# Soft-MoE on a gated recurrence: the combine's turned logits in SBUF, their difference on GpSimd, fewer fillers, and new orders

## The chip, the cores and the metric

One NeuronCore of a Trainium2 chip runs the whole kernel as one launch. The metric is the device time of one execution in microseconds (us). Before the change it is 282.06 us, the median of three runs (281.35 to 282.72). PE is TensorE, DVE is VectorE, ACT is ScalarE, POOL is GpSimd, SP is SyncE.

## What is computed

All arrays are float32. The first half is a gated linear recurrence over 4 sequences of 5056 tokens with 256 channels; the second is a soft mixture of 8 experts with 4 slots each over all 20224 tokens.

```
log_a   = 8 * sigmoid(r_gate) * log(clip(sigmoid(a_param), 1e-6, 1 - 1e-6))
a       = exp(log_a)
h[t]    = a[t] * h[t-1] + sqrt(max(1 - a[t]^2, 1e-6)) * sigmoid(i_gate[t]) * x[t]     # y = h, restarted for each sequence
logits  = y @ phi                                   # 20224 x 32
d       = exp(logits - max over tokens) ; d /= sum over tokens + 1e-9
slots   = d.T @ y                                   # 32 x 256, 4 rows to an expert
out_e   = relu(slots_e @ w1_e) @ w2_e               # hidden width 1024
c       = exp(logits - max over slots) ; c /= sum over slots + 1e-9
result  = c @ out                                   # 20224 x 256
```

## The kernel before, in words

The tokens are cut into quads of 512 (the last of 256), numbered 0 to 39. A unit is what one load brings: quad 0 alone, then pairs of quads, and quad 39 alone; 21 units, 0 to 20. A group, of which there are 12, is two units (groups 0 to 8) or one (9 to 11). r_gate comes with channels on partitions, x and i_gate with tokens on partitions. Nearly all of SBUF is one array, `all_s`, of 48 slots, which the program's allocator gives out; beside it there are four buffers `yn` for the recurrence's output with tokens on partitions. PSUM's eight banks are two single banks and three pairs, and eight single banks once the last pairs are free.

Every step is a task with a name, made of a few letters and a number: a load `Dr3`, `Di3` or `Dx3` of unit 3; `SR` and `SI`, the gates' sigmoids, as hyperbolic tangents (ScalarE); `EX`, the exponential that makes a (ScalarE); `SQ`, its square (GpSimd or VectorE); `RT`, the root (ScalarE); `U`, the product of input gate and x (GpSimd or VectorE); `TU`, its turn into PSUM (PE); `ST`, times the root, and `SC`, the scan (VectorE); `TY`, the turn of the scan's output (PE) and `YC`, its copy to `yn` (ScalarE or VectorE); `LG`, the logits (PE); `LE`, their copy with a running maximum (VectorE); `LD`, `TE`, `ES`, the difference, its turn and its exponential; `AC`, the sum over tokens on PE, `DM` and `AE`, its correction to a new maximum. A letter per quad in the string `IV` says how U is made: D is one operation on VectorE, (i + 1) * x; E is the plain product i * x, and TU then turns both the product and x into the same bank, which adds them; P adds 1 to i on GpSimd first.

Behind the last group stands the merge: the maxima are turned and joined (`MT`, `MX`, `MR`, `MC`), the weights of the partial sums made (`WJ`, `WE`, `W`), and the slots computed (`SP`, copied by `SL`, L1281). The experts follow: `L1.0` to `L1.7`, the first product of each expert (PE, L1320), `HS`, `HT`, `HR`, the relu with a turn, in two halves; `L20.x` and `L21.x`, the second product for either half of the channels (PE, L1368); `SO` (L1386), `RS` (L1391) and `SW` (L1395), the output rows scaled, spread over the partitions and copied.

The combine runs on each group g: `CT` turns blocks of the logits on VectorE (L1428), `CM` takes the maximum over the slots (L1439), `CS` subtracts it (L1442), `CE` is the exponential (ScalarE, L1445), `RR`, `RB`, `RC` make the reciprocal of the sum (L1457 to L1459), `CN` multiplies by it (GpSimd, L1462), and `HE` turns the result back (VectorE, L1484). Then for each half of the channels, u = 2g and 2g + 1: `OT` (PE, L1498), its copies `OE` from PSUM (ScalarE L1512 or VectorE L1514), and the transfer `OD` out (SyncE, L1525). In the kernel before, CT writes to a PSUM bank.

The order of the work on every engine is written out as a list of task names for each, and one list, B, for the order in which buffers are taken. A planner walks through these lists with an estimated duration for each task and emits the instructions; at run time every engine works through its own in that order and waits on semaphores. Where the planner sees PE idle, between two given times (`WARMF` and `WARMT`), it puts in a filler: two transposes of the identity that no one reads (L1206). SyncE issues all loads and outputs; `a_param` alone is loaded from ScalarE's queue (L678). The program's functions that the change touches are these:

Of the kernel before, what the change touches and what calls it, by code (L numbers as in the profile page):

```python
# [15 lines left out]
P = 128  # L16
# [10 lines left out]
IV = 'DDDEEEEEEEDEEEEEEEEEEEEEEDEEEEPPEPPPPPPP'  # L27
# [12 lines left out]
WARMT = 245.0  # L40
# [37 lines left out]
GATES0 = False  # L78
# [19 lines left out]
    ),  # L98
    "ACT": (
# [11 lines left out]
    ),  # L111
# [43 lines left out]
COLDX = 1.9  # L155
IDLE = 2.8
CHILL = 5.0
LOAD = 1.41

EXG = 2  # L160

MI = ()
SI2 = ()
RT2 = ()
XFER = 1.265
ISSUE = 0.4
FIRST = 0.7
REACH = 2.6
REACHO = 1.55
LATO = 1.75  # L170
LATL = 1.1
DEEP = 8
PEX = 1.03

ODS = 0
OHALF = 1

# [373 lines left out]
def kernel(  # L551
# [11 lines left out]
    nc = tc.nc if tc is not None else None  # L563
# [6 lines left out]
    QT = J * P  # L570
# [72 lines left out]
    add = planner.add  # L643
# [493 lines left out]
    def exs(p):  # L1137

        return [] if p < first_of[p][-1] else [("EX", first_of[p][0], h) for h in range(H)]
# [464 lines left out]
```

## Time and profile before

| what | value |
|---|---|
| median of 3 runs | 282.06 us (281.35 to 282.72) |
| the profiled execution's own time | 281.48 us |
| its span, first to last instruction | 279.3 us |
| mean granted PE clock | 0.936 of full |
| busy: PE, DVE, ACT, POOL | 237.8, 235.3, 234.0, 181.2 us |
| HBM read, written | 78.94 MB, 20.71 MB |
| chain that ended last | PE 25%, POOL 24%, DVE 19%, ACT 12%, DMA 9%, issue 6% |

The span cut into 40 equal slices of 7 us, each digit the busy share in tenths (PEclk: the granted clock in tenths of full speed):

```profile
PE   8979688777699798798998999999999999989910
...
DVE  0066999999989999999999999999999999986420
ACT  6799999999999999999999999998823388697420
POOL 5102979999999999899999999998210430222000
PEclk9999799979979989999999999999999999999555
DMA  7999999999999969939699999999940069999995
```

A busy time is that of an engine's instructions; matmuls overlap, so PE's is no measure of its peak. The span holds the loads and the recurrence (to about 205 us), the merge and the experts (to about 222), and the outputs.

### The profile page before, as it was taken

How to read it: one execution, taken by the hardware profiler on the slowest of the kernel's cores; microseconds unless marked ns; L12 is line 12 of the kernel's file. 1: busy time of each engine (PE TensorE's matmuls, PEld its weight loads, DVE VectorE, ACT ScalarE, POOL GpSimd, SP SyncE). 2: the span in 40 equal slices, each digit the busy share in tenths (PEclk: the TensorE clock that was granted, in tenths of full speed). 3: DMA queues.
4: the chain of work that ended last, by engine and by line, in shares of the span. 5: the costliest groups of instructions: out<-in, count | busy, mean ns of one | idle time of the engine just before them, and what ended most of it. 6: DMA issues, size and time to landing. Idle time of an engine off the chain costs nothing.

```text
span 279.3 us, 5879 instructions
## 1 busy us (share of the span) xinstructions
PE 237.8 (85%) x2405; PEld 178.9 (64%) x2405; DVE 235.3 (84%) x279; ACT 234.0 (84%) x237; POOL 181.2 (65%) x143
## 2 busy tenths in 40 slices
PE   8979688777699798798998999999999999989910
PEld 8979576655476686476766776857665766545600
DVE  0066999999989999999999999999999999986420
ACT  6799999999999999999999999998823388697420
POOL 5102979999999999899999999998210430222000
PEclk9999799979979989999999999999999999999555
DMA  7999999999999969939699999999940069999995
GB/s 255 412 422 422 422 414 420 421 420 425 392 422 418 428 248 422 427 113 407 223 400 374 391 395 413 414 407 428 419 170 2 2 238 415 411 425 420 406 413 246
DMA packets 15562, 100.02 MB, mean 358 GB/s; under 512 B 1968, under 2 KB 2480, under 8 KB 4144
## 3 DMA queue, kind: packets, MB, share of 16 engines
q1 hardware_dynamic: 15392, 99.65, 87.7%
q8 instruction: 19, 0.31, 0.4%
q14 instruction: 7, 0.06, 0.0%
q10 hardware_dynamic: 144, 0.00, 0.0%
HBM read 78.94 MB, written 20.71 MB: 357 GB/s over the span
## 4 chain that ended last, share of the span: by engine, by line
PE 25%; POOL 24%; DVE 19%; ACT 12%; DMA 9%; issue 6%; SPq 0%; ACTq 0%; DVEq 0%; POOLq 0%
POOL all_s L822 10%; POOL all_s L839 10%; DVE all_s L920 10%; DVE pair L903 6%; PE bank L1498 5%; DMA all_s<-in_x_dram 4%; PE pair L943 3%; POOL all_s L810 3%; ACT all_s L854 3%; DMA out_dram<-all_s 3%; DMA all_s<-in_r_gate_dram 3%; PE bank L1206 3%; PE bank L1320 3%; PE pair L885 2%; ACT all_s L800 2%
## 5 line engine op out<-in xcount | busy, mean ns | idle before, releaser
L920 DVE TENSOR_TENSOR_SCAN all_s<-all_s,pair 128x1024 f32<-128x1024 f32 (+8 forms) x48 | 92.8, 1950 | 0.7
L822 POOL TENSOR_TENSOR all_s<-all_s 128x1024 f32<-128x1024 f32 (+1 forms) x35 | 81.4, 2348 | 4.5 <-ACT all_s L800 3.1
L839 POOL TENSOR_TENSOR all_s<-all_s 128x1024 f32<-128x1024 f32 (+2 forms) x36 | 66.9, 1878 | 22.6 <-ACT all_s L854 21.8
L885 PE MATMUL pair<-ident,all_s 128*128 128x128 f32 x524 | 69.1, 286 | 11.5 <-DVE all_s L920 7.0
L885 PEld LDWEIGHTS pair<-ident,all_s 128*128 128x128 f32 x524 | 60.5, 146 | 22.8 <-DVE all_s L920 9.2
L903 DVE SCALAR_TENSOR_TENSOR pair<-all_s,pair 128x1024 f32<-128x1024 f32 (+2 forms) x42 | 48.0, 1151 | 3.8 <-ACT all_s L868 2.1
L943 PE MATMUL pair<-ident,all_s 128*128 128x128 f32 x312 | 42.1, 279 | 6.1 <-DVE all_s L920 4.7
L943 PEld LDWEIGHTS pair<-ident,all_s 128*128 128x128 f32 x312 | 34.3, 141 | 14.6 <-DVE all_s L920 6.8
L854 ACT ACTIVATE all_s<-all_s,ca 128x2048 f32<-128x2048 f32 (+3 forms) x24 | 42.2, 1788 | 0.1
L1462 POOL TENSOR_TENSOR all_s<-all_s,rs_all 128x512 f32<-128x512 f32 (+3 forms) x12 | 10.8, 905 | 47.4 <-DVE rs_all L1459 19.5
L785 ACT ACTIVATE all_s<-all_s 128x2048 f32<-128x2048 f32 (+2 forms) x21 | 37.5, 1804 | 1.7 <-DMA all_s<-in_r_gate_dram 1.6
L800 ACT ACTIVATE all_s<-all_s 128x2048 f32<-128x2048 f32 (+2 forms) x21 | 37.4, 1802 | 0.0
L868 ACT ACTIVATE all_s<-all_s 128x2048 f32<-128x2048 f32 (+2 forms) x21 | 36.7, 1803 | 0.1
L1512 ACT COPY all_s<-bank 128x512 f32<-128x512 f32 (+2 forms) x41 | 21.2, 555 | 10.1 <-PE bank L1498 4.7
L1206 PE MATMUL one<-ident 128*128 128x128 f32 x160 | 28.4, 295 | 1.4 <-POOL ident masks.py:199 1.4
L1498 PE MATMUL bank<-lD,all_s 32*128 32x512 f32 (+3 forms) x114 | 25.6, 650 | 1.4 <-DVE lD L1484 0.8
L1004 PE MATMUL one<-all_s,phi_sb 128*32 128x256 f32 (+1 forms) x320 | 23.3, 386 | 2.7 <-DVE all_s L1020 2.4
L1079 PE MATMUL one<-yn,eS 128*32 128x257 f32 x296 | 21.7, 388 | 1.8 <-ACT eS L1060 1.8
L1206 PEld LDWEIGHTS one<-ident 128*128 128x128 f32 x160 | 21.3, 153 | 2.1 <-POOL ident masks.py:199 1.4
L957 ACT COPY yn<-pair 128x1024 f32<-128x1024 f32 x21 | 21.0, 1006 | 1.1 <-PE pair L943 1.1
L959 DVE COPY yn<-pair 128x1024 f32<-128x1024 f32 x18 | 21.7, 1208 | 0.1
L1514 DVE COPY all_s<-bank 128x512 f32<-128x512 f32 (+3 forms) x27 | 15.0, 574 | 6.9 <-PE bank L1498 2.8
(115 smaller groups left out, 297.8 us busy)
## 6 DMA issues: line engine op xcount, KB each, us to landing
all_s<-in_r_gate_dram SPq DMA_DIRECT2D x19, 1024.0 KB, 10.8
all_s<-in_i_gate_dram SPq DMA_DIRECT2D x19, 1024.0 KB, 16.1
all_s<-in_x_dram SPq DMA_DIRECT2D x19, 1024.0 KB, 10.1
all_s<-in_moe_w_dram SPq DMA_DIRECT2D x16, 1024.0 KB, 9.5
out_dram<-all_s SPq DMA_DIRECT2D x16, 1024.0 KB, 7.1
out_dram<-all_s SPq DMA_DIRECT2D x4, 512.0 KB, 6.2
all_s<-in_r_gate_dram SPq DMA_DIRECT2D x3, 256.0 KB, 2.9
out_dram<-all_s SPq DMA_DIRECT2D x2, 384.0 KB, 4.7
```

The costliest lines, as they stand in the source:

```text
L785: nc.scalar.activation(v, v, AF.Tanh, scale=0.5)
L800: nc.scalar.activation(v, v, AF.Tanh, scale=0.5)
L822: eng.tensor_tensor(out=o, in0=a, in1=b, op=ALU.mult)
L839: eng.tensor_tensor(out=t(Nb[(p, h)])[:, :c], in0=v, in1=v, op=ALU.mult)
L854: nc.scalar.activation(v, v, AF.Exp, scale=ca[:, h : h + 1], bias=ca[:, h : h + 1])
L868: nc.scalar.activation(v, v, AF.Sqrt, bias=f, scale=-f)
L885: nc.tensor.matmul(t(up)[:, i, m * P : (m + 1) * P], raw(nm, q)[:, m * D + h * P : m * D + (h + 1) * P], ident, is_transpose=True, start=( ...
L903: nc.vector.scalar_tensor_tensor(v, w, 1e-3 if gate_of(quads(p)[0]) == "S" else 0.5e-3, v, op0=ALU.max, op1=ALU.mult)
L920: nc.vector.tensor_tensor_scan(dst, dst, flat()[:, s0:s1], init, op0=ALU.mult, op1=ALU.add)
L943: nc.tensor.transpose(out=flat()[:, b * D + h * P : b * D + (h + 1) * P], in_=t(A[p])[:, h, i * QT + (b0 + b) * P : i * QT + (b0 + b + 1) ...
L1206: nc.tensor.transpose(out=t(b)[:, 0, :P] if b.tag == "pair" else t(b)[:, :P], in_=ident, identity=ident)
L1498: nc.tensor.matmul(t(op)[:, :w], t(soRb[h])[r, :P], t(hT)[r, :w], start=True, stop=True)
```

## The change

It does six things. The turned logits of the combine go to one of the four `yn` buffers, once quad 39 has taken its own, and no longer to a PSUM bank. Their difference to the maximum, CS, is done by GpSimd. The load of `a_param` is issued by SyncE, ahead of all other loads. Fillers are put in up to a planned 60 us instead of 245. Quads 1 and 10 use form E of U instead of D. And all lists are new; the planner's estimates for the first loads and for the preparation of the parameter are other numbers, and its two tasks SA and LN are one.

```diff
-IV = 'DDDEEEEEEEDEEEEEEEEEEEEEEDEEEEPPEPPPPPPP'
+IV = 'DEDEEEEEEEEEEEEEEEEEEEEEEDEEEEPPEPPPPPPP'
...
-WARMT = 245.0
+WARMT = 60.0
...
-FIRST = 0.7
+FIRST = 1.05
...
-        nc.scalar.dma_start(out=ca, in_=a_param.rearrange("(p h) -> p h", p=P))
+        nc.sync.dma_start(out=ca, in_=a_param.rearrange("(p h) -> p h", p=P))
...
-                          prio=p, emit=emit, alloc=[b], lat=LATL if p else 0.05)
+                          prio=p, emit=emit, alloc=[b], lat={"r0": -0.25, "i0": 0.9, "r3": 1.7, "r1": 1.4, "r2": 1.4}.get(f"{nm}{p}", LATL if p else 0.05))
...
-    t_sa = add("ACT", "SA", 0.2 if GATES0 else 2.95, prio=-90, kind="ln" if GATES0 else "", deps=[t_const], emit=e_sa)
-
-    t_ln = add("ACT", "LN", 0.2 if GATES0 else 1.5, prio=-90, kind="ln" if GATES0 else "", lat=0.13 if GATES0 else -1.2, emit=e_ln, deps=[t_sa])
+    t_ln = add("ACT", "SA", 3.65, prio=-90, kind="", lat=-1.2, deps=[t_const], emit=lambda: (e_sa(), e_ln()))
+
...
-        cp = Buf(ONE, f"cp{g}")
+        cp = Buf("yn", f"cp{g}")
+        cp.late = last_y
...
-        k = add("DVE", f"CS{g}", 0.1 + 0.5 * L / QT, deps=[k, LD[g]], prio=pc, uses=[cp, rm, lSb[g // 2]],
-                emit=lambda: nc.vector.tensor_tensor(
+        k = add("POOL", f"CS{g}", 0.1 + 0.91 * L / QT, deps=[k, LD[g]], prio=pc, uses=[cp, rm, lSb[g // 2]],
+                emit=lambda: nc.gpsimd.tensor_tensor(
```

Of the lists, the stretches that the prediction speaks of, before (-) and after (+):

```
DVE, start
-  CA SQ3.1 SQ3.0 SQ0.0 U0 SQ1.0 SQ2.0 U2 U1 ST0.1 ST0.0 SC0.1 SC0.0 ST1.0 ...  SQ6.1 SC3.0 YC1.0 U10 ST4.1
+  CA SQ0.1 SQ3.0 SQ0.0 U2 U1 SQ2.0 U0 ST0.1 SC0.1 ST0.0 SC0.0 ST1.1 ...  YC1.0 SQ7.0 SQ5.1 ST4.0
DVE, merge and combine
-  LE10 LE11 LD10 MX LD11 AE9 MR YC38.0 CT2 WJ AE10 W AE11 CM2 CT0 SL CM0 CT4 CT5 CT1 CT3 CS0 CM1 RD CS2 CS1 ...
+  LE10 LE11 LD10 CT2 MX CM2 MR AE9 LD11 WJ CT1 CT11 W AE10 AE11 CM1 SL RR2 CT0 CT4 CM11 CM0 CT3 CT8 CM4 RR1 CM3 HS0 CM8 RD HR0 ... HE1 RC2 RC3 CT6 CM6 HE0 SW0 ...
ACT, start
-  SA LN SR0 EX0.1 EX0.0 SR3 EX3.0 SR1 EX3.1 SR2 SI0 EX1.0 SI1 SI2 EX1.1 RT0.0 RT3.0 RT1.0 RT2.0
+  SA SR0 EX0.0 EX0.1 SR3 EX3.0 SR1 SR2 EX3.1 EX1.0 SI1 SI2 SI0 EX1.1 RT0.0 RT3.0 RT1.0 RT2.0
ACT, merge
-  ES9 ES11 ES10 YC39.0 DM11 DM10 WE CE0 HS0
+  ES9 YC39.0 DM10 ES10 YC38.0 WE ES11 DM11 CE2 CE11
PE, merge to outputs
-  MT TY38.0 TE10 TE11 TY39.0 MC AC10.0 ... L20.7 L21.0 L21.1 RS0 L21.2 OT0 L21.3 L21.4 OT2 L21.5 L21.6 L21.7 OT4 RS1 OT1 OT3 ... OT18 OT20 OT19 OT21 OT17 OT22 OT16 OT23
+  MT TY39.0 TE10 TY38.0 MC TE11 AC10.0 ... L20.7 L21.0 RS0 L21.1 OT0 L21.2 OT2 L21.3 L21.4 OT4 L21.5 L21.6 L21.7 OT6 RS1 OT3 ... OT20 OT21 OT18 OT19
POOL
-  const const2 SQ0.1 SQ1.1 SQ2.1 U3 U4 ...  SQ4.1 LD0 SQ7.1 SQ6.0 SQ7.0 SQ5.1 U9 ... PD9 HZ PD11 SZ PD10 CN1 CN0 CN2
+  const const2 SQ3.1 SQ1.0 SQ1.1 SQ2.1 U3 U4 ...  LD0 SQ5.0 SQ4.1 SQ7.1 SQ6.0 SQ6.1 U10 U9 ... PD9 HZ PD10 PD11 CS2 SZ CS1 CS11 CS0 CS4 CS3 CN1 CN0 CN3 CN2
SP, start
-  Dr0 Dr3 Dr1 Dr2 Di0 Di1 Dx0 Di2 Dx1 Dx2
+  Dr0 Dr3 Dr1 Dr2 Di2 Di1 Dx1 Di0 Dx2 Dx0
```

## Rows read from the trace of the kernel before

**Rows 1.** Windows of the core: stretch, length, PE, PEld, DVE, ACT, POOL busy, clock, DMA.

```profile
20.00:40.00 20.00, 16.34 (x130) 15.86 (x131) 16.95 (x14) 19.94 (x13) 12.04 (x6) 0.91 1.02 421
...
60.00:80.00 20.00, 15.58 (x130) 10.90 (x129) 18.43 (x17) 19.97 (x12) 19.46 (x9) 0.85 1.01 411
...
160.00:180.00 20.00, 19.12 (x194) 14.86 (x193) 19.73 (x18) 19.78 (x18) 20.00 (x14) 1.00 1.00 402
...
240.00:250.00 10.00, 9.16 (x67) 4.68 (x66) 9.02 (x20) 8.03 (x20) 2.73 (x4) 1.00 1.01 417
```

**Rows 2.** Timeline of the start: start, length, engine, line, operation, idle before.

```profile
0.73 2.30 SPq L731 DMA_DIRECT2D all_s<-in_r_gate_dram  x5
0.76 0.39 ACTq L678 DMA_DIRECT2D ca<-in_a_param_dram  x1
...
9.54 1.92 ACT L785 ACTIVATE all_s<-all_s 128x2048 f32<-128x2048 f32 x1 [1.59 <-DMA all_s<-in_r_gate_dram]
```

**Rows 3.** Lines by form: u's product and the square, on GpSimd and on VectorE.

```profile
L822 POOL TENSOR_TENSOR all_s<-all_s 128x1024 f32<-128x1024 f32 x34 | 80.1, 2379 | 4.5 <-ACT all_s L800 3.1 <-DMA all_s<-in_x_dram 1.4
...
L839 POOL TENSOR_TENSOR all_s<-all_s 128x1024 f32<-128x1024 f32 x33 | 64.6, 1980 | 18.4 <-ACT all_s L854 17.6 <-PE pair L943 0.7
...
L839 DVE TENSOR_TENSOR all_s<-all_s 128x1024 f32<-128x1024 f32 x5 | 6.6, 1360 | 11.2 <-ACT all_s L854 11.2
L820 DVE SCALAR_TENSOR_TENSOR all_s<-all_s 128x1024 f32<-128x1024 f32 x5 | 6.5, 1322 | 2.4 <-DMA all_s<-in_x_dram 2.4
```

**Rows 4.** Timeline of the merge on VectorE: quad 38's copy and the slot copy.

```profile
204.23 1.21 DVE L959 COPY yn<-pair 128x1024 f32<-128x1024 f32 x1
...
208.68 0.22 DVE L1281 COPY yn<-one 128x64 f32<-128x64 f32 x1
```

**Rows 5.** Windows of the fillers' line alone (L1206): stretch, length, PE, PEld, clock, DMA.

```profile
60.00:200.00 140.00, 0.00 (x0) 0.00 (x0) 0.97 0.94 378
...
207.00:228.00 21.00, 1.65 (x10) 0.91 (x9) 1.00 0.10 38
228.00:246.00 18.00, 9.19 (x70) 7.54 (x70) 1.00 0.99 407
```

**Rows 6.** Timeline around the first output.

```profile
221.95 0.27 ACT L1395 COPY all_s<-bank 128x128 f32<-128x128 f32 x1 [0.64 <-PE bank L1391]
...
222.42 0.44 PE L1206 MATMUL bank<-ident 128*128 128x128 f32 x2
...
222.78 0.93 PE L1498 MATMUL bank<-lD,all_s 32*128 32x384 f32 x8
...
223.64 1.08 PE L1368 MATMUL one<-all_s 128*32 128x128 f32 x32
...
224.65 7.59 SPq L1525 DMA_DIRECT2D out_dram<-all_s  x5
...
224.66 0.71 PE L1498 MATMUL bank<-lD,all_s 32*128 32x512 f32 x3
```

**Rows 7.** Windows of one microsecond after the first output's transfer has begun.

```profile
225.00:226.00 1.00, 1.00 (x20) 0.28 (x16) 0.87 (x4) 0.94 (x4) 0.76 (x1) 1.00 0.61 216
...
227.00:228.00 1.00, 1.00 (x20) 0.31 (x8) 1.00 (x4) 0.68 (x2) 0.00 (x0) 1.00 0.46 169
228.00:229.00 1.00, 1.00 (x10) 0.76 (x7) 1.00 (x2) 0.63 (x2) 0.98 (x1) 1.00 0.64 267
```

**Rows 8.** Lines by form: the combine's steps on 512 columns.

```profile
L1462 POOL TENSOR_TENSOR all_s<-all_s,rs_all 128x512 f32<-128x512 f32 x8 | 8.4, 1049 | 36.9 <-DVE all_s L1353 14.6 <-DVE rs_all L1454 9.9 <-DVE rs_all L1459 9.0
...
L1484 DVE STREAM_TRANSPOSE lD<-all_s 128x512 f32<-128x512 f32 x6 | 4.1, 690 | 1.4 <-PE bank L1498 1.4
...
L1442 DVE TENSOR_TENSOR all_s<-bank,rm 128x512 f32<-128x512 f32 x6 | 4.0, 674 | 0.0
L1428 DVE STREAM_TRANSPOSE bank<-all_s 128x512 f32<-128x512 f32 x6 | 3.9, 695 | 0.0
```

**Rows 9.** Window of the output matmuls alone (L1498) after the last filler, at the lower clock.

```profile
257.00:268.00 11.00, 8.60 (x44) 6.35 (x42) 0.51 1.01 410
```

More of the change, by code (lines that the diff above doesn't have):

```diff
@@ L1159 @@
         if not k and not GATES0:
-            phases = [[("SA",), ("LN",)]] + phases
+            phases = [[("SA",)]] + phases
         elif not k:
             phases = [merge([("SR", q) for q in cq[0] + ahead], [("SI", q) for q in cq[0] if not late_i(q)])]
-            phases.append([("SA",), ("LN",)] + [e for p in chunks[0] for e in exs(p)])
+            phases.append([("SA",)] + [e for p in chunks[0] for e in exs(p)])
         if k >= QL and k > 0:
@@ L1200 @@
         mk_group(g)
-    kinds = {"SR": SR, "SI": SI, "EX": EX, "RT": RT, "SA": {(): t_sa}, "LN": {(): t_ln}}
+    kinds = {"SR": SR, "SI": SI, "EX": EX, "RT": RT, "SA": {(): t_ln}}
     seq = [kinds[it[0]][it[1] if len(it) == 2 else it[1:]] for ph in phases for it in ph if it[0] != "X"]
```

111 rows, old and new, of the table ORDER are left out of this document.

## The prediction

> **What bounds the kernel now.** I read the page's busy shares first, then the windows, then the chain of waits, and last the timeline of the start, of the merge and of the first output.
>
> The shares hide three stages. From the first wide sigmoid at 9.54 [rows 2] to the last root, near 197, three engines are full at once: ScalarE is busy 19.94, 19.97 and 19.78 of 20 us in the stretches at 20, 60 and 160 us, VectorE and GpSimd 19.73 and 20.00 in the last of them [rows 1]. The DMA runs at its limit for most of this, yet its loads only wait for free slots. ScalarE has no idle time to give back, so whatever starts it later moves everything. The second stage is a serial chain: merge the maxima, the slots (SL, ending at 208.90 [rows 4]), then the experts' matmuls, with PE never idle, to the first output matmul OT0 at 222.78 [rows 6]. The third is DMA alone: 20.71 MB of output at the 417 GB/s of the stretch at 240 us [rows 1] are 49.7 us, and the transfers begin at 225.4, since 0.61 of the window at 225 is used [rows 7]. So the end is the first output's transfer, plus 49.7 us, plus every hole in the DMA behind it. There is one such hole: 0.54 us unused in the window at 227 and 0.36 at 228, together 0.90 [rows 7].
>
> **The change, part by part.** Its sum is made against the profiled execution: span 279.3, 281.48 in all, 0.58 below the median of 282.06. Differences are then put on the median.
>
> *Decay's parameter first.* Its transfer leaves ScalarE's queue, where it took 0.39 us beside a table load, and goes to the head of SyncE's. Behind it there stand all the loads; five r issues took 2.30 us, 0.46 each [rows 2]. ScalarE waited 1.59 us for the second r load and began at 9.54 [rows 2]; from there it is full. One issue later is 0.4 us later for all of them. Bounds: 0, if the shared transfers and not the issue set that landing, and 0.46. I take **+0.4**. What it gains (the exponential of the parameter earlier) ends before that wait and is worth nothing. The Trainium skill (DMA: Bandwidth & Descriptors, Issuing engines are not separate DMA queues) says that a second issuing engine saves only the sequencer's time, usually small beside the transfer; by it the move would cost the same issue slot, and the row of five issues agrees, since here that slot stands ahead of a transfer that is waited for.
>
> *Products and squares on other engines.* U1 and U10 become the plain product, whose sum with x is made by eight more transposes on PE, for U1 where fillers run anyway. U10 leaves VectorE (1.32) for GpSimd (2.38) [rows 3]. Against it, one wide square more of units 4 to 7 goes to VectorE (SQ7.0 and SQ5.1 in place of SQ6.1): 1.36 there, 1.98 less on GpSimd [rows 3]. VectorE's net is +0.04, GpSimd's +0.40. GpSimd is busy 19.46 of 20 us where U10 falls [rows 1], so 0.54 us hides part of it. Early, two wide squares go to GpSimd, which was idle 7.96 us of the stretch at 20 [rows 1]: free. Bounds: 0 to +0.4; taken **+0.2**. If the cover were gone, the price is that of the third rival.
>
> *Turned logits in SBUF.* The buffer moves from a PSUM bank to one of the four yn slots, of which the slots' tile takes one. The turn to SBUF costs what the one to PSUM does: the existing turn between two SBUF tiles is 690 ns, the one to a bank 695 [rows 8]. So 0, plus or minus 0.1 for all. Three free slots let three groups be in flight; the banks it frees make room for output matmuls.
>
> *The difference on GpSimd.* VectorE loses 12 subtractions of up to 674 ns, 6.9 us over all widths; GpSimd gains 12 at what its products of the same shape take, 1049 ns, 10.8 us over all widths [rows 8]. GpSimd has done little there: 2.73 us of 10 even at 240 [rows 1]. Each group's chain is 0.37 us longer, but a group of 512 columns feeds two outputs, 5 us of DMA. Only the first two groups stand near the path, and in the new list their differences run before SL ends or beside the experts' 11 us. I take 0 (bounds -0.4 to +1.0: the second if CN0 is late behind six differences of 1.05 in GpSimd's order and HE0, next to SW0 on VectorE, holds OT0). The Trainium skill (GPSIMD Engine Reference, Performance versus the Vector engine) puts such an add on GpSimd at 1.96 times VectorE's time; the rows here make it 1.56, and by that section the twelve would be some 13.5 us, as an estimate, still beside other work.
>
> *The merge in the new lists.* Quad 38's copy, 1.21 us on VectorE between the maxima and SL [rows 4], goes to ScalarE. In its place the turn and maximum of groups 2, 1 and 11 stand there, 0.70 and 0.67 us each [rows 8] for the wide ones, some of them in the gaps in which VectorE waits for PE. Behind them wait WJ, W, AE11 and then SL. I take **+0.1** (bounds -0.5 to +0.8).
>
> *Fillers in the first quarter alone.* None ran between 60 and 200 us; 10 recorded matmuls lie in 207 to 228 and 70 in 228 to 246 [rows 5]. The last ones lie under the DMA and cost nothing. One pair is on the path: it starts at 222.42, SW0 (ScalarE) has ended at 222.22, and OT0 begins behind the pair at 222.78 [rows 6]. **-0.36.**
>
> *Order of the first outputs.* RS0 now stands behind one step of L21 instead of two, OT0 behind two instead of three, OT2 behind three instead of five. Two such steps took 1.08 us [rows 6]. OT0 hangs on RS0 and SW0 as well, so I count 0.15 there; between OT0 and OT2 one step less, 0.54, comes out of the hole of 0.90. **-0.7** together.
>
> Sum: 0.4 + 0.2 + 0.1 - 0.36 - 0.7 = -0.36 us. On the profiled execution 281.1, on the median **281.7**.
>
> **The rivals.**
>
> *First, faster: the new order also takes out idle time.* VectorE is idle 3.05 us in the stretch at 20 and 1.57 at 60, where the clock is granted at 0.85 of full [rows 1], so that PE works at 1.2 GHz for part of it, and VectorE waits for its transposes. If the new lists keep half of the 1.57, and the whole hole of 0.90 closes, and the load issue costs nothing: -0.8 - 0.90 - 0.36 - 0.15 = -2.2, so 279.9. For it: VectorE stood at 9.02 of 10 us as late as 240 and now has 6.9 less. Against: ScalarE is full all the same.
>
> *Second, slower: PE cannot feed the DMA without fillers.* With none behind 228, PE has only the output matmuls, and its clock may fall early. In 257 to 268, at 0.51, it was busy 8.60 us [rows 9] for the outputs 19, 21, 17, 22, 16 and 23 of the list, in all 3328 KB, and perhaps half of output 20, 3584 KB: 2.46 to 2.65 us for each 1024 KB, and the DMA takes 2.51 at 417 GB/s [rows 1]. Once PE takes longer than that, the end follows PE: over the 17 times 1024 KB left at 232, 0.14 us each at most, 2.4 us. With the gains ahead of it, 284.1. Against: the DMA stayed at 1.01 in that very stretch [rows 9], and narrow forms dear in PE time were among its matmuls. The Trainium skill (TensorE: Matmul & The Clock Gate, HAM oscillation) says that pauses between bursts bring the gate down and that each burst then starts at half clock; the 0.51 after the last filler agrees, and the consequence in time is this rival's.
>
> *Third, slower: the main stage grows.* GpSimd takes U10 whole (+2.38) without the square counting back [rows 3], as the two need not fall in one wait; U0's sigmoid now stands behind those of units 1 and 2, so the first scan starts later. GpSimd is full, 20.00 of 20 us, in the stretch at 160 [rows 1]. +2.4 + 0.4 - 1.06 = +1.7: 283.8. It decides once GpSimd's last product of u ends later than ScalarE's last root. Against: VectorE's idle 3.05 us in the stretch at 20 [rows 1] covers a late first scan.
>
> **How the numbers follow.** Within 0.5%, 1.4 us, is what a measurement here cannot tell from no change. Forecast 0.47 (own range 280.6 to 282.9), first rival 0.29, second 0.08, third 0.16. Faster by more than 0.5%: 0.04 of the forecast, all of the first but 0.01, and 0.02 of the others, 0.34. Slower: 0.03 of the forecast, 0.07 of the second and 0.11 of the third, 0.21. The rest, 0.45, is no change. The range reaches to the first rival with the whole 1.57 idle gone (279.1) and to the second: 279.1 to 284.0.
>
> **What would show it.** Start: ScalarE's second sigmoid at 9.9 instead of 9.54. Main: ScalarE's last root some 0.6 later, GpSimd full. Merge: SL still some 6 us behind the last scan. Fillers: no L1206 after 60 us, OT0 at most 0.2 us behind SW0. Outputs: the hole in the DMA under 0.4 us. Combine: the differences around 1.05 us on GpSimd, HE0 done before SW0. DMA at 1.0 from 232 to 275, whatever the clock. The forecast is wrong if GpSimd or VectorE waits for long in the main stage, if HE0 holds OT0, or if the DMA share falls below 0.95 in a window behind 232.

## The result, and the profile after

The changed kernel takes 286.88 us, the median of ten runs (283.36 to 290.45), against 281.54 for the kernel before in the same comparison (ten runs, 279.99 to 283.00). The ratio is 1.0141, 95% interval 1.0094 to 1.0189, or 4.0 us (2.6 to 5.3): slower, and outside the range that was given. Four of the ten runs, the profiled one among them, are over 1.5% above the fastest and count as slow; here and below, a median is of all runs and a ratio of the others alone. The profiled execution took 289.43 us in all (span 287.6), so a second profile, of a shorter execution of the same kernel and called the repeat below (283.69 us, span 281.9), is read beside it, and what only the long one shows is named as such.

The windows of the changed kernel, columns as in [rows 1]:

```profile
20.00:40.00 20.00, 16.85 (x142) 16.61 (x141) 13.71 (x11) 19.91 (x14) 13.54 (x7) 0.91 1.02 421
60.00:80.00 20.00, 14.21 (x128) 11.44 (x128) 19.93 (x15) 19.20 (x12) 19.24 (x10) 0.91 0.96 387
...
240.00:250.00 10.00, 8.03 (x52) 4.01 (x45) 10.00 (x23) 9.24 (x21) 3.50 (x5) 1.00 1.01 413
```

ScalarE was full at 60 us before [rows 1]. In the long execution it is VectorE, 19.93 of 20 us, and ScalarE has 0.80 to spare. In the repeat ScalarE is full and VectorE nearly so, where it had 1.57 to spare before:

```profile
60.00:80.00 20.00, 15.57 (x141) 12.73 (x139) 19.61 (x18) 19.96 (x12) 18.32 (x10) 0.91 1.02 423
```

The chain of waits points the same way in its shares by engine; before, they were PE 25%, GpSimd 24%, VectorE 19%. After, in the long execution and in the repeat:

```profile
DVE 42%; PE 29%; DMA 9%; issue 9%; ACT 5%; POOL 1%; SPq 0%; DVEq 0%; ACTq 0%; POOLq 0%
DVE 34%; PE 17%; DMA 16%; ACT 12%; issue 8%; POOL 6%; SPq 2%; DVEq 0%; ACTq 0%; POOLq 0%
```

Pieces of that chain in the long execution (start, length, what):

```profile
10.05 17.40 DMA all_s<-in_x_dram
27.55 2.26 DVE all_s L821
...
63.37 3.34 DVE all_s L840
...
129.29 2.34 DVE all_s L821
...
206.70 1.82 POOL all_s L1302
```

The first line is the wait for x0, three are VectorE instructions that take 1.22 us undisturbed (U0, the square SQ5.1, and U25), and the last is GpSimd's memset HZ, in the middle of VectorE's path. The stages side by side, in us, each read from the timelines (SR3 is ScalarE's second sigmoid):

```
                SR3   first ST  last scan ends  SL      OT0     first output issued  span
before          9.54  28.40     201.73          208.68  222.78  224.65               279.3
after          10.06  31.93     210.60          218.17  231.67  233.53               287.6
after, repeat  10.12  31.19     205.52          213.09  226.59  228.46               281.9
```

From SL on, the change does what it was forecast to: SL to OT0 takes 13.50 instead of 14.10, and from the first output's issue to the end 54.1 and 53.4 instead of 54.65. All that is lost lies ahead of SL. In the long execution it is 9.5 us: 3.53 up to the first ST, 5.34 from there to the last scan, 0.62 in the merge. In the repeat it is 4.4: 2.79, 1.00 and 0.62.

The middle term can be counted on VectorE. Between the first ST and the last scan of the long execution, U25 took 3.21 (before 1.56 us), LD9 1.79 (0.33), the two squares 1.22 and 3.42 where before a square and U10 took 1.91 and 1.39, and idle time is 0.86 more: 1.65 + 1.46 + 1.34 + 0.86 = 5.31. In the repeat U25 took 3.41 and LD9 1.78, 1.85 and 1.45 more; the squares took 1.21 and 1.22, together 0.87 less than the square and U10 before; and idle time is 1.26 less: 1.85 + 1.45 - 0.87 - 1.26 = 1.17. There the two long instructions are partly made up for by less waiting. The square's 3.42 stands in the long execution alone. Ahead of the first ST, U0 took 2.25 and 2.27 for 1.23. So the question is why the same instruction takes 1.22 us once and 3.42 the next time. Rows of the kernel before, VectorE beside GpSimd, round U25 (L820) and LD9 (L1040):

```profile
123.66 1.90 POOL L839 TENSOR_TENSOR all_s<-all_s 128x1024 f32<-128x1024 f32 x1
...
125.08 1.56 DVE L820 SCALAR_TENSOR_TENSOR all_s<-all_s 128x1024 f32<-128x1024 f32 x1
...
198.92 0.33 DVE L1040 TENSOR_SCALAR lD<-all_s,M 128x256 f32<-128x256 f32 x1
...
199.12 1.87 POOL L1302 MEMSET all_s<- 128x2048 f32 x1 [2.11 <-DVE all_s L920]
```

The same two places in the repeat of the changed kernel (lines are one higher):

```profile
125.98 0.69 POOL L1037 TENSOR_SCALAR lD<-all_s,M 128x512 f32<-128x512 f32 x1
126.65 1.89 POOL L840 TENSOR_TENSOR all_s<-all_s 128x1024 f32<-128x1024 f32 x1
...
126.21 3.41 DVE L821 SCALAR_TENSOR_TENSOR all_s<-all_s 128x1024 f32<-128x1024 f32 x1
...
201.62 1.81 POOL L1302 MEMSET all_s<- 128x2048 f32 x1 [2.11 <-DVE all_s L921]
...
201.79 1.78 DVE L1041 TENSOR_SCALAR lD<-all_s,M 128x256 f32<-128x256 f32 x1
```

Add starts and lengths. Before, GpSimd's square ends at 125.56 and U25 at 126.64, 1.08 later. In the repeat GpSimd's second instruction ends at 128.54 and U25 at 129.62, again 1.08 later. LD9 began 0.20 ahead of the memset HZ before, and 0.17 behind its start after; it then ended 0.14 behind HZ's end. A VectorE instruction with its operands in SBUF that meets a running GpSimd instruction waits for its end, and the wait stands in the profile as a long instruction, not as idle time. Theory from here on: the loss is mostly such holds, and the new orders place VectorE's few products, squares and LD9 where they meet more of them. Rival: the late first scan (x0 landed 17.40 us after its issue) moves the whole stage. A second rival: the load of decay's parameter, the edits of the combine, or the fillers.

A long instruction need not be a late end. What LD9's hold costs stands in the distance from the end of ScalarE's last root to the end of the last scan: 4.80 to 4.98 us in the ten profiles of this document in which LD9 was not held, 6.24 to 6.39 in the four in which it was.

The Trainium skill (SBUF — State Buffer, "SBUF: two separate sides") says that VectorE and GpSimd share one pair of ports as an exclusive lock held for a whole instruction, so that the loser blocks. The sums above agree; the lock itself stands in no row.

### The profile page after: what moved, and what is told of

Read it like the earlier page. It is cut to its first block, busy times and chain, and to the rows that moved or that the text cites. A ratio compares the mean times of both kernels' runs of the same rounds, so it can differ in the third digit from the quotient of the medians.

```text
span 287.6 us, 5822 instructions
## 1 busy us (share of the span) xinstructions
PE 237.2 (82%) x2371; PEld 180.1 (63%) x2371; DVE 236.0 (82%) x273; ACT 232.9 (81%) x230; POOL 194.9 (68%) x156
## 4 chain that ended last, share of the span: by engine, by line
DVE 42%; PE 29%; DMA 9%; issue 9%; ACT 5%; POOL 1%; SPq 0%; DVEq 0%; ACTq 0%; POOLq 0%
DVE all_s L921 18%; DVE pair L904 12%; PE pair L886 9%; DMA all_s<-in_x_dram 6%; PE bank L1499 6%; DVE yn L960 3%; PE pair L944 3%; DMA all_s<-in_r_gate_dram 3%; PE bank L1368 3%; PE bank L1320 3%; PE one L1499 2%; DVE all_s L1515 2%; ACT all_s L1513 2%; PE one L1005 2%; DVE all_s L1021 2%
## 5 line engine op out<-in xcount | busy, mean ns | idle before, releaser
L886 PE MATMUL pair<-ident,all_s 128*128 128x128 f32 x540 | 73.0, 293 | 19.7 <-DVE all_s L921 13.5
L823 POOL TENSOR_TENSOR all_s<-all_s 128x1024 f32<-128x1024 f32 (+1 forms) x36 | 85.4, 2395 | 2.9 <-ACT all_s L801 2.1
L886 PEld LDWEIGHTS pair<-ident,all_s 128*128 128x128 f32 x540 | 65.7, 151 | 27.8 <-issue 15.0
L840 POOL TENSOR_TENSOR all_s<-all_s 128x1024 f32<-128x1024 f32 (+1 forms) x36 | 66.1, 1852 | 23.3 <-ACT all_s L855 20.8
L944 PE MATMUL pair<-ident,all_s 128*128 128x128 f32 x316 | 42.7, 278 | 5.5 <-DVE all_s L921 4.5
L944 PEld LDWEIGHTS pair<-ident,all_s 128*128 128x128 f32 x316 | 34.3, 140 | 16.1 <-DVE all_s L921 7.5
L1513 ACT COPY all_s<-bank 128x512 f32<-128x512 f32 (+3 forms) x44 | 21.4, 537 | 13.7 <-PE bank L1499 10.0
L1206 PE MATMUL one<-ident 128*128 128x128 f32 x140 | 26.5, 289 | 1.4 <-POOL ident masks.py:199 1.4
L958 ACT COPY yn<-pair 128x1024 f32<-128x1024 f32 (+1 forms) x23 | 22.5, 987 | 5.2 <-DVE yn L1429 3.1
L1499 PE MATMUL bank<-lD,all_s 32*128 32x512 f32 (+3 forms) x100 | 22.6, 669 | 3.5 <-DVE lD L1485 2.0
L1463 POOL TENSOR_TENSOR all_s<-all_s,rs_all 128x512 f32<-128x512 f32 (+3 forms) x12 | 10.7, 906 | 19.4 <-DVE rs_all L1460 18.9
L1005 PE MATMUL one<-all_s,phi_sb 128*32 128x256 f32 (+1 forms) x320 | 22.7, 380 | 0.1
L1206 PE MATMUL pair<-ident 128*128 128x128 f32 x106 | 21.4, 285 | 0.0
L960 DVE COPY yn<-pair 128x1024 f32<-128x1024 f32 x17 | 20.5, 1211 | 0.9 <-PE pair L944 0.8
## 6 DMA issues: line engine op xcount, KB each, us to landing
all_s<-in_i_gate_dram SPq DMA_DIRECT2D x19, 1024.0 KB, 14.1
```

Source lines behind the costliest of these rows:

```text
L823: eng.tensor_tensor(out=o, in0=a, in1=b, op=ALU.mult)
L840: eng.tensor_tensor(out=t(Nb[(p, h)])[:, :c], in0=v, in1=v, op=ALU.mult)
L886: nc.tensor.matmul(t(up)[:, i, m * P : (m + 1) * P], raw(nm, q)[:, m * D + h * P : m * D + (h + 1) * P], ident, is_transpose=True, start=( ...
L944: nc.tensor.transpose(out=flat()[:, b * D + h * P : b * D + (h + 1) * P], in_=t(A[p])[:, h, i * QT + (b0 + b) * P : i * QT + (b0 + b + 1) ...
L1206: nc.tensor.transpose(out=t(b)[:, 0, :P] if b.tag == "pair" else t(b)[:, :P], in_=ident, identity=ident)
L1499: nc.tensor.matmul(t(op)[:, :w], t(soRb[h])[r, :P], t(hT)[r, :w], start=True, stop=True)
```

## Experiments

Every run is compared with the kernel before on the same chip; ratios are to that kernel, with 95% intervals.

**The changed kernel again, and with its start put back.** The first is unaltered. The second has the old order of the first loads and products:

```diff
-Dr0 Dr3 Dr1 Dr2 Di2 Di1 Dx1 Di0 Dx2 Dx0
+Dr0 Dr3 Dr1 Dr2 Di0 Di1 Dx0 Di2 Dx1 Dx2
...
-SQ0.0 U2 U1 SQ2.0 U0 ST0.1
+SQ0.0 U0 SQ2.0 U2 U1 ST0.1
...
-SR2 EX3.1 EX1.0 SI1 SI2 SI0
+SR2 EX3.1 SI0 EX1.0 SI1 SI2
```

> The changed kernel once more, unaltered, for a second profile of it. Two theories for its 9 us at the end of the main stage in the profiled execution. Late x: unit 0's x load stands behind five other loads, U0 starts at 27.55 instead of 19.60 and the first ST at 31.93 instead of 28.40; the loss is made there and is in every execution, 2.5 to 3.5 us. Blocked port: instructions of VectorE with two SBUF inputs, or plain SBUF operations, that meet one of GpSimd are held until it ends (U0 2.25 us, SQ5.1 3.42, U25 3.21, LD9 1.79 against 1.2 to 1.6 and 0.33 undisturbed, 6 us together); which ones meet hangs on the moment, so they differ between executions and make the spread of 283 to 290. Late x alone expects 284 to 285 with the same first ST at 31.9; blocked port expects another set of long instructions in an execution of another length.

> The changed kernel with the order of the first loads (Di0 Di1 Dx0 Di2 Dx1 Dx2), of SI0 on ScalarE (ahead of EX1.0) and of U0 on VectorE (ahead of SQ2.0, U2, U1) as before the change; all else as changed. Late x: the first ST is back at 29 and the time falls by 2.5 to 3.5 us, to about 282. Blocked port: the first ST is earlier too, but what is gained there is lost where instructions meet GpSimd's; the time falls by less than 1 us and its spread stays at several us.

Measured: 285.55 us, ratio 1.0111 (1.0073 to 1.0149), and 285.51, 1.0144 (1.0094 to 1.0193). The first ST came back to 28.38, in part because ScalarE's second sigmoid was early there, at 8.16: behind it the first ST lies 20.2 us, against 21.1 in the repeat and 18.9 before. Yet the time did not fall: U25 took 3.79, SQ7.0 1.75, U0 2.46, and the last scan ended at 204.55. The late x0 is real, but putting it right bought nothing here.

**Fillers, and the combine, each alone on the kernel before.**

```diff
-WARMT = 245.0
+WARMT = 60.0
```

> The kernel before with fillers up to a planned 60 us only. My step: one filler pair less ahead of OT0, -0.36 us (281.2), and the DMA share stays at 1.0 from 232 on although the clock falls earlier. Rival: PE at 1.2 GHz can't feed the DMA, +1 to +2.4 us with a DMA share under 0.95 in some window behind 232.

```diff
-        cp = Buf(ONE, f"cp{g}")
+        cp = Buf("yn", f"cp{g}")
+        cp.late = last_y
...
-        k = add("DVE", f"CS{g}", ...   nc.vector.tensor_tensor(
+        k = add("POOL", f"CS{g}", ...  nc.gpsimd.tensor_tensor(
```

> The kernel before with the combine's part of the change alone: turned logits in the yn buffers and CS on GpSimd (the twelve CS taken out of VectorE's list and put among GpSimd's CN in the order CS0 CS2 CS1 CS3 CN1 CN0 CS5 CS4 CS6 CN2 ...). My step: 0 (-0.4 to +1.0). Rival: with three buffers for the turned logits VectorE waits for GpSimd's CS before it can go on with its list, HE0 and with it OT0 come later, +1 to +3 us.

Fillers alone: 281.36, ratio 0.9995 (0.9966 to 1.0025); SL to OT0 13.7 instead of 14.1, the 0.4 of the filler pair. The combine alone, on the old lists: 285.61, ratio 1.0170 (1.0125 to 1.0215). Its turn of group 3 finds no free buffer until the experts' first product has read the slots:

```profile
215.96 0.71 DVE L1429 STREAM_TRANSPOSE yn<-all_s 128x512 f32<-128x512 f32 x1 [4.66 <-PE bank L1320]
```

HE0 stands behind it on VectorE, and behind one more wait of 2.29 us for GpSimd's differences, and begins 18.0 us after SL instead of 12.7. In the changed kernel's lists, where turns and differences alternate, HE0 begins 12.2 after SL: there the combine costs nothing.

**LD9 put back in the changed kernel, and put wrong in the kernel before.**

```diff
-SC19.1 AE8 LD9 ST20.0     # changed kernel
+SC19.1 LD9 AE8 ST20.0
...
-SC19.1 LD9 AE8 ST20.1     # kernel before
+SC19.1 AE8 LD9 ST20.1
```

> The changed kernel with LD9 and AE8 exchanged back in VectorE's list (LD9, AE8, as before). Theory (held by GpSimd): a VectorE instruction that has all its operands in SBUF and begins while GpSimd is inside an instruction waits until that instruction ends. In the unaltered changed kernel LD9 began 0.17 us into GpSimd's memset HZ (1.81 us) and took 1.78 us; before the change it began 0.21 us ahead of it and took 0.33. So LD9 takes 0.33 us here, the last scan ends 1.4 us earlier behind the same first scan (length from the first ST to the last scan 172.9 us instead of 174.3), and the time is 1.4 us less: 284.1. Rival (LD9 waits for its own data, the maxima of group 9, or only takes the place of another wait): LD9 may be short, but the last scan ends where it did, and the time stays at 285.5.

> The kernel before with only AE8 and LD9 exchanged in VectorE's list (AE8, LD9), the order of the changed kernel at this one place. Theory (held by GpSimd): LD9 now begins some 0.1 to 0.2 us behind the start of GpSimd's memset HZ, and takes 1.8 us instead of 0.33; the last scan, SL and the end all come 1.4 us later: 282.9. Rival: the order of two instructions of 0.3 us does nothing, 281.5, and LD9 stays at 0.33.

In the kernel before, the exchange of two short instructions gave 282.89 us, ratio 1.0030 (1.0001 to 1.0060), so between 0 and 1.7 us more. Its timeline:

```profile
199.08 1.81 POOL L1302 MEMSET all_s<- 128x2048 f32 x1 [2.11 <-DVE all_s L920]
...
199.25 1.78 DVE L1040 TENSOR_SCALAR lD<-all_s,M 128x256 f32<-128x256 f32 x1
```

The start was the same as before to 0.01 us, the last scan ended at 203.11, 1.38 later, and SL came 1.39 later. The theory holds at this place. In the changed kernel LD9 came back to 0.33 and the stage from first ST to last scan to 172.7, but the median fell only to 285.10 (1.0121, 1.0073 to 1.0169), not to 284.1, no gain that the times can tell; in its profile U25 took 3.89.

**Start, LD9 and U25 together.** The edits of start and LD9, and one on GpSimd, so that U25 meets one square only:

```diff
-LD4 SQ13.0 LD3 SQ14.0 SQ14.1
+LD4 LD3 SQ13.0 SQ14.0 SQ14.1
```

> The changed kernel with three edits of order: the first loads and products as before (as in the run that restored the start alone), LD9 ahead of AE8, and on GpSimd LD3 moved one place forward (LD4 LD3 SQ13.0 SQ14.0), so that VectorE's product U25 no longer begins in the last half us of the short LD3 but inside a square. Theory (held by GpSimd): U25 took 3.4 to 3.8 us in three runs of the changed lists because it lost the port twice, to LD3 and to the square behind it; with one square running it takes at most 1.9 + 1.1 = 3.0 and about 1.6 where the square is near its end, as before the change (1.56). Forecast: U25 1.2 to 2.4, LD9 0.33, the last scan 1.4 + 1.5 = 2.9 us earlier than with the start alone (204.55), so at about 201.7, where it was before the change; time 285.5 - 2.9 = 282.6, and with the merge still 0.6 longer and the output part 1.2 shorter, level with the kernel before (281.5). Rival (the new lists of the main stage are slower by their order of products and squares as a whole): the last scan ends at 204 or later and the time stays above 284.

284.48 us, ratio 1.0097 (1.0063 to 1.0130): the forecast failed. U25 took 3.20 all the same. GpSimd's square ended 0.26 us after U25 began, the next square went first, and U25 ended 1.08 after that one. And TensorE's granted clock fell to 0.83 and 0.60 in the two 3 us stretches around SL, which put HE0 13.8 us behind SL instead of 12.2. One more thing is read from this pair of runs: with the late start of the previous run the first ST is at 32.33 and the last scan ends at 205.00; here they are 29.62 and 204.88. VectorE was idle 1.24 us between the two there and 4.21 here. ScalarE's last root ended at 200.20 there and at 200.07 here, and the last scan 4.8 us behind it in both. The late first scan is given back.

**Old lists to the last scan, new ones behind it.** On the kernel before:

```diff
 DVE ... SC20.1 LE10 LE11     # as before up to here; the changed kernel's list follows
+LD10 CT2 MX CM2 MR AE9 LD11 WJ CT1 CT11 W AE10 AE11 CM1 SL ...
 ACT ... YC37.0 ES9           # PE is joined behind MT, GpSimd behind U39, SP ahead of OD0.0
+YC39.0 DM10 ES10 YC38.0 WE ES11 DM11 CE2 ...
-WARMT = 245.0
+WARMT = 60.0                 # and the combine's edits
```

> The kernel before with its own lists up to the last scan (start, main stage, LD9 ahead of AE8, decay's parameter on ScalarE's queue), and behind it the changed kernel's lists for the merge, the combine and the outputs, with the turned logits in SBUF, their difference on GpSimd, and fillers in the first quarter alone. Theory (the loss is all in the start and the main stage, the gain all behind the slots): last scan 173.3 us behind the first ST as before; SL some 0.6 us later (merge 7.15 instead of 6.5); from SL to OT0 13.5 instead of 14.1; outputs 53.5 instead of 54.5 for the closed hole in the DMA. Sum 0.6 - 0.6 - 1.0 = -1.0: 280.5. Rival (the output lists only fit the main stage they were planned with, or the combine on GpSimd costs behind SL): SL to OT0 14 us or more, or the time at 281.5 or above.

281.26 us, ratio 0.9990 (0.9957 to 1.0023): with the old main stage the loss is gone, though the gain expected did not show. HE0 began 13.8 us behind SL. The windows of this kernel there (PE busy is the first figure behind the length, the clock the third from the end):

```profile
208.00:211.00 3.00, 2.62 (x34) 1.73 (x38) 2.58 (x7) 0.00 (x0) 1.06 (x2) 0.83 0.03 8
211.00:214.00 3.00, 3.00 (x40) 1.62 (x36) 2.76 (x5) 0.83 (x2) 1.54 (x3) 0.60 0.00 0
```

**Fillers kept until just behind SL; and a shorter merge.** Both are the joined kernel (the expectations call it mixed). The second also moves the turns and maxima of groups 1 and 11 behind SL, those of group 2 behind AE9 and WJ, and LD11 ahead of MR; ScalarE's and PE's lists of the merge change with it and are not shown:

```diff
-WARMT = 60.0
+WARMT = 213.0     # both
...
-LE11 LD10 CT2 MX CM2 MR AE9 LD11 WJ CT1 CT11 W AE10 AE11 CM1 SL
+LE11 LD10 MX LD11 MR AE9 CT2 WJ CM2 W AE10 AE11 SL CT1 CT11 CM1
```

> The mixed kernel (old lists to the last scan, new ones behind it) with the fillers kept until just behind SL, none under the outputs. In the mixed kernel without them TensorE's granted clock was 0.83 and 0.60 in the two 3 us stretches that follow SL - 0.9, its first L2 matmul began 9.4 us behind SL and HE0 13.8; in the changed kernel and two of its variants the clock was 1.00 there and the same steps took 7.7 and 12.2. Theory (the clock falls in some executions because the new merge leaves TensorE gaps that fillers filled before): clock 1.00 in the merge, SL to HE0 12.2, and the median 0.8 to 1.6 below that of the mixed kernel (281.3): 279.7 to 280.5, which is below the kernel before. Rival (the clock there does not depend on the fillers): the profile shows either clock, and the median stays at 281.3.

> As the mixed kernel with fillers until SL, and in the merge the turns and maxima of groups 1 and 11 moved behind SL, LD11 ahead of MR (so that it does not meet GpSimd's difference CS2, which held it 0.5 us), the copy of quad 38 still on ScalarE. Theory (VectorE's order in the merge sets SL): SL 6.3 to 6.7 us behind the start of LE11 instead of 7.1, HE0 no later, so 0.3 to 0.8 below the kernel with fillers until SL: 279.4 to 280. Rival (the chain through TensorE, ScalarE and the last quad's copy sets SL, or the turns moved behind SL then hold HE0): no gain, or HE0 later than 12.2 us behind SL.

With the fillers: 280.13 us, ratio 0.9933 (0.9905 to 0.9960), below both kernels, as expected. The same two stretches:

```profile
207.00:210.00 3.00, 3.00 (x48) 2.15 (x49) 2.58 (x7) 0.00 (x0) 1.05 (x1) 1.00 0.00 0
210.00:213.00 3.00, 3.00 (x60) 1.80 (x56) 2.77 (x5) 0.83 (x2) 1.50 (x3) 1.00 0.00 0
```

HE0 is 12.2 behind SL again. The shorter merge missed: 282.45, ratio 1.0046 (1.0021 to 1.0071), SL 8.3 behind LE11 instead of 7.15. Now it is W (L1265, 0.23 us undisturbed) that meets the difference CS2 on GpSimd, and the memset behind it:

```profile
206.55 1.05 POOL L1443 TENSOR_TENSOR all_s<-yn,rm 128x512 f32<-128x512 f32 x1 [3.93 <-ACT eS L1060]
206.75 1.39 DVE L1265 TENSOR_SCALAR W<-R,wj 128x128 f32<-128x128 f32 x1 [0.35 <-ACT wj L1264]
207.53 0.53 POOL L1240 MEMSET yn<- 128x512 f32 x1
```

And HE0 came 13.8 us behind SL at full clock, because the copy that feeds HT0 queued behind the turns that had been moved.

**Decay's parameter alone on the kernel before.**

```diff
-        nc.scalar.dma_start(out=ca, ...
+        nc.sync.dma_start(out=ca, ...
```

> The kernel before with only decay's parameter loaded from the head of SyncE's queue instead of ScalarE's. Theory (the prediction's step): all loads are issued one slot of 0.46 us later, ScalarE's second sigmoid begins 0.4 to 0.5 later, and so does everything behind it: 281.3 + 0.4 = 281.7. Rival (the shared transfers set the landing, or VectorE's scans set the pace and the slot is hidden): the second sigmoid moves by less than 0.2 and the time stays at 281.3. A difference of 0.4 is below what the timing tells; the trace decides, by the start of ScalarE's sigmoids.

282.38 us, ratio 1.0047 (1.0022 to 1.0071): 1.3 us by the ratio and not 0.4; the medians differ by 0.8. ScalarE's timeline: the first sigmoid is earlier than before (4.73 for 5.34), the second later than in [rows 2]:

```profile
4.73 1.06 ACT L785 ACTIVATE all_s<-all_s 128x1024 f32<-128x1024 f32 x1 [0.46 <-DMA all_s<-in_r_gate_dram]
...
10.31 1.91 ACT L785 ACTIVATE all_s<-all_s 128x2048 f32<-128x2048 f32 x1 [2.97 <-DMA all_s<-in_r_gate_dram]
```

**The changed kernel repaired.** The old start and LD9 ahead of AE8 as above, and

```diff
-AE2 U25 YC13.0 ST11.1
+AE2 YC13.0 U25 ST11.1
...
-WARMT = 60.0
+WARMT = 213.0
```

> The changed kernel with what the other runs point to undone, its lists otherwise kept: the first loads and products in the old order, LD9 ahead of AE8, U25 one place later (behind YC13.0), fillers until just behind SL. Theory (late first scan, VectorE held by GpSimd at U25 and LD9, and TensorE's clock in the merge are the whole loss): U0 1.23, first ST 18.9 us behind ScalarE's second sigmoid, LD9 0.33, U25 at most 2.7, last scan 173 to 174.5 us behind the first ST, SL to HE0 12.2: 281.3 + 0.5 for the load issue + 0.7 in the main stage + 0.6 in the merge - 1.4 behind SL = 281.7. Rival (something else in the new lists costs, as GpSimd's own order): 283 or more.

282.09 us, ratio 1.0012 (0.9993 to 1.0031): level with the kernel before, and 0.4 from what was expected. U25, one place later, begins 0.76 ahead of GpSimd's next square and takes 1.22; that square now waits instead, 2.21 for 1.96:

```profile
126.83 1.96 POOL L840 TENSOR_TENSOR all_s<-all_s 128x1024 f32<-128x1024 f32 x1
129.65 2.21 POOL L840 TENSOR_TENSOR all_s<-all_s 128x1024 f32<-128x1024 f32 x1 [0.87 <-ACT all_s L855]
...
128.90 1.22 DVE L821 SCALAR_TENSOR_TENSOR all_s<-all_s 128x1024 f32<-128x1024 f32 x1
```

LD9 took 0.33, HE0 began 12.2 behind SL, and the last scan ended 174.0 us behind the first ST. One step missed: U0 met a square and took 2.57, not 1.23, and the first ST came 20.1 us behind the second sigmoid, not 18.9. Three edits of order and the fillers undo the loss. Which share each has in the median was not separated further.

U25's share is smaller than its hold. It took 1.98 less here than in the run with start, LD9 and U25 together. VectorE was 0.58 us ahead of that run at AE2, the last instruction ahead of both places, and 1.19 ahead at the next scan, so 0.6 came through: the copy that now stands ahead of U25 waits for PE.

```profile
127.75 1.23 DVE L960 COPY yn<-pair 128x1024 f32<-128x1024 f32 x1 [1.29 <-PE pair L944]
```

## Why the prediction was wrong

The step that failed is the one for the main stage, "products and squares on other engines", taken at +0.2. It priced the instructions that change engines, each at the mean of its form, 1322 and 1360 ns [rows 3], and put the new order of all others at nothing, without a reason. The moved ones were not the loss: "VectorE's net is +0.04", and in the repeat it was -0.87 (+1.34 in the long execution). U25 and LD9, which lost, stay on VectorE and only change place. The means could not show it. They mix undisturbed instructions of 1.22 us with held ones: before, the five squares were four of 1.22 and SQ6.1 of 1.91. A held product or square takes the rest of what GpSimd is doing when it comes, and 1.08 us more. In the changed lists the excess was +1.6 to +2.3 for U25 in five of five profiles that left it in its place, +1.45 for LD9 in four of four with AE8 ahead of it, and +2.2 for SQ5.1 in the profiled execution alone (1.22 in the repeat). The last may also bear on the wide spread: SQ5.1 began 0.71 us behind the start of a long product there and 0.45 ahead of one in the repeat. The sign named in advance, a long wait of VectorE or GpSimd, could not show this, since a held instruction counts as busy.

How much of it reached the end is known in part. LD9's hold did, 1.4 us. U25's did for 0.6 us where it can be compared. Besides, ScalarE's last root ended 189.2 to 190.2 us behind the start of its second sigmoid in five profiles with the changed lists of the main stage (194.3 in the long execution) and 187.2 to 189.1 in eight with the old ones. U25's hold does not explain that: it was 189.3 in the repaired kernel too, where U25 took 1.22. The cause stays open.

Decay's parameter was forecast at +0.4, with 0.46 as the upper bound: direction right, mis-sized, 1.3 (0.6 to 2.0) measured by the ratio. One issue slot was counted. But in seven profiles with the parameter on ScalarE's queue the second sigmoid began at 7.92 to 9.54 us, 8.45 in the mean, and in seven with it on SyncE's at 8.16 to 10.69, mean 9.91. The landing of the second r load has early cases, near 8, and late ones from 9.5 on: two late ones of seven before, six of seven behind the extra slot. The single profile of before showed a late case, 9.54, and looked like the norm. What decides between them was not tried. The Trainium skill (DMA: Bandwidth & Descriptors, "Issuing engines are not separate DMA queues") says that a second issuing engine saves only the sequencer's time, usually small beside the transfer. By it the move is worth one slot, 0.46 us; the run shows more, 0.6 at least, and the measurement decides.

The third rival had the direction, and its late first scan happened (3.53 us). Its price of 1.7 was too small and its place wrong: GpSimd was not the bound, since its last product ended 3.5 us ahead of ScalarE's last root (3.2 in the repeat), and the late scan is nearly all given back. The argument against it was half right. Of the 3.05 us idle in the stretch at 20 [rows 1], 2.9 lie ahead of the first ST, which is at 28.40; the idle time that covers a late first scan lies behind it, 4.21 us in the run with the early start and 1.24 in the one with the late.

The first rival, idle time taken out, came in part in the repeat, where VectorE idled 1.26 us less between the first ST and the last scan (0.86 more in the long execution); the holds took more than that. Its reading of the 1.57 us at 60 [rows 1] was half right: 0.92 waited for PE's turns and 0.61 for a root of ScalarE.

The merge: +0.62 for +0.1, inside its bounds; 0.52 of it is LD11, held 0.81 for 0.29 by the same difference CS2 that the change put on GpSimd.

Behind SL the steps held. The filler pair and the order of the first outputs: SL to OT0 -0.60, forecast -0.51. The outputs: 0.6 less from first issue to end in the long execution and 1.2 in the repeat, forecast 0.54. The windows after the first transfer, answering [rows 7], in the long execution:

```profile
234.00:235.00 1.00, 1.00 (x35) 0.81 (x32) 1.00 (x4) 0.98 (x3) 1.00 (x2) 1.00 0.65 247
235.00:236.00 1.00, 1.00 (x20) 0.32 (x9) 1.00 (x3) 0.33 (x1) 0.30 (x1) 1.00 0.40 151
236.00:237.00 1.00, 1.00 (x32) 0.72 (x32) 1.00 (x2) 0.55 (x2) 0.41 (x1) 1.00 0.94 372
```

The hole is 0.60 + 0.06 = 0.66 us there instead of 0.90. In the repeat it is 0.03 + 0.07 = 0.10, below the 0.4 that the prediction named:

```profile
230.00:231.00 1.00, 1.00 (x16) 0.31 (x8) 1.00 (x3) 0.25 (x1) 0.21 (x1) 1.00 0.97 381
231.00:232.00 1.00, 1.00 (x34) 0.80 (x34) 1.00 (x3) 0.63 (x2) 0.49 (x1) 1.00 0.93 375
```

The second rival (PE too slow without fillers) did not happen. In the long execution the clock was 0.50, the lower of its two levels (1.2 GHz), from 256 to 264 and again from 272, and the DMA stayed full:

```profile
256.00:258.00 2.00, 1.75 (x8) 0.17 (x1) 0.48 (x1) 0.97 (x3) 0.00 (x0) 0.50 0.98 406
258.00:260.00 2.00, 1.02 (x5) 0.58 (x9) 1.80 (x5) 0.00 (x0) 0.00 (x0) 0.50 1.04 434
```

Where the missing fillers can cost is ahead of that, in the merge, which the prediction left out: none was counted there because they were not on the path. Turned logits in SBUF and the difference on GpSimd cost 0 at the path behind SL as forecast, by grace of the new lists; on the old ones they cost 4.8 us (3.5 to 6.1) together.

## What to carry to other kernels

Where VectorE and GpSimd are both full, look at every VectorE instruction that works SBUF to SBUF on the timeline of both engines, and price it by what it will meet, not by the mean of its form: the spread within a form is the price of the holds. A new order of a full stage is a change of its own; if a change brings one, run its lists by halves, as the joined kernel did: the gain lay in one half, the loss in the other. Where an instruction was held, ask what the instruction behind it would have waited for anyway. And a wait ahead of the first work should be read from more than one profile.

## What the runs showed of the hardware

A held VectorE product or square of 1.22 us ended 1.08 or 1.09 us after the end of a GpSimd instruction in all 35 cases of the 14 profiles; of the other 113, two began inside a GpSimd instruction, with 0.13 and 0.16 us of it left, and none of the rest did. It can lose more than once: in the five profiles with U25 in its changed place GpSimd's instruction had 0.17 to 0.47 us left when U25 began, and the next one, or the next two, went first; with the old lists 0.32 to 0.96 were left in six profiles, and U25 went next in all. What decides is not shown. A memset, which has no input, held a subtraction from one array in SBUF (LD9, 0.33 us) in four profiles; it ended 0.14 or 0.15 after the memset.

TensorE's clock behind SL, with the new merge and no fillers, stayed at 1.00 in four profiles and fell in two, to 0.60 in the mean of 3 us (its levels are 0.5 and 1.0 of full), though PE had been busy alike in the 3 us round SL (2.61 in the run with LD9 alone, at 1.00, and 2.62 in the joined kernel, at 0.83). With fillers until SL it was 1.00 in all three. HE0 came 1.6 us later in both profiles with the fall.
